# Seeding a second accumulation by a PSUM-to-PSUM copy in a seven-product matmul kernel

## The chip, the cores and the metric

The kernel runs on one core of one Trainium2 chip. The metric is the device time of one execution in microseconds (us). The engines are PE (TensorE, matrix products), DVE (VectorE), ACT (ScalarE), POOL (GpSimd) and SP (SyncE, which here only issues DMAs). PE writes its products to PSUM, a small memory of eight banks per partition, from which DVE and ACT read them.

## The reference, cut to what matters

A linear attention gives x of 4608 tokens by 512. Two blocks follow, each with its own float64 weights of 512 x 2048 and 2048 x 512:

```python
def _moe_ref(x, w_in, w_out):
    h = x @ w_in
    r = np.maximum(h, 0.0)
    return (r * r @ w_out).astype(np.float32)

def _moe2_ref(x, w_in, w_out):
    h = x @ w_in
    return ((h * np.cos(h)) @ w_out).astype(np.float32)
```

## The kernel before, in words

Every product is made of three PE passes: each operand is split into a high and a low part, and high x high, high x low and low x high are summed in PSUM. A first stage (up to 499 us) does the attention and one half of the first block in plain tiles. The second stage is a list of 30 `slots`, numbered k = 0 to 29 in the order of work. A slot is (m, t, q): m is the block (0 or 1), t one of five token tiles, q a group of hidden features. Tiles 0 to 2 have 2 x 512 tokens and tiles 3 and 4 have 2 x 384. Slots 0 to 9 belong to block 0 (two groups a tile), slots 10 to 29 to block 1 (four groups a tile). Slots 10, 14, 18, 22 and 26 begin a new tile of block 1 (q = 0), and the input blocks of the tile are made around them.

In a slot the product x @ w_in is done as seven products of 2 x 2 blocks instead of eight (`first_product`, indices i of `ORDER` = 0, 1, 3, 2, 5, 4, 6, each of 12 matmuls). They go to two double banks, `FA` and `FB`, of 128 x 2 x 512 float32: 0, 3, 5 and 6 to one, 1, 2 and 4 to the other, the roles changing from slot to slot. Some accumulate on what the bank holds: 3 on 0, 5 on those, 4 on 2. Block (0, 0) of h is product 0 plus product 1: ACT copies product 0 to SBUF (`keep`, tile `m`) and DVE adds product 1 from the other bank (`add`, L530 or L534). The four blocks then go through a chain that ACT and DVE share (`relu_1`, `relu_2`, or `cos_1` to `cos_5`). The last block, (1, 0), comes from product 6 at the slot's end.

The result of the chain is multiplied by w_out, again by seven products in most slots (`second_product`, banks `SA` and `SB`, matmuls of 256 columns in block 1, 24 of them to a product in tiles of 2 x 512 tokens and 18 in tiles of 2 x 384). Their order is `S_ORDER`. `s_block` makes the operand of each: a difference of blocks where needed (tiles `t`), then the high part `gh` on ACT and the low part `gl` on DVE. `drain_product` adds each product to a sum in SBUF: at q = 0 of block 1 four of them by an ACT copy that starts the sum, otherwise by a DVE add (L700), and products 4, 5, 1 and 6 (`BY_DMA`) by an ACT copy to one of two `part` buffers and a DMA that adds it to the sum (L697, L698). The second products of slot k run 1.25 slots after its first ones, so PE alternates between first products of slot k + 1 and second products of slot k.

`run_slots` sets the order by a clock of steps: step n issues one matmul of the first products, and as many of the second products as are due at n/84 slots. All other work hangs in a list of jobs by position (`at(pos(...))`, unit PH = 1/7 slot), and a scheduler puts each engine's instructions in a queue that it works off in order.

Of the kernel before, what the change touches and what calls it, by code (L numbers as in the profile page):

```python
# [8 lines left out]
F32 = mybir.dt.float32  # L9
# [13 lines left out]
def kernel(  # L23
# [15 lines left out]
    nc = tc.nc  # L39
# [390 lines left out]
    ORDER = (0, 1, 3, 2, 5, 4, 6)  # L430
    W_OF = (0, 1, 3, 4, 6, 5, 2)
    BLOCKS = {(0, 0): 2, (1, 1): 5, (0, 1): 6, (1, 0): 7}
    S_ORDER = (0, 2, 3, 4, 5, 1, 6)
    BY_DMA = (4, 5, 1, 6)
    xb, wi, wo, kept, hs, ys, sums, quads = {}, {}, {}, {}, {}, {}, {}, {}

    def big(pool, dtype, name, ht):
# [62 lines left out]
    def first_product(k, i):  # L500
        m, t, q = slots[k]
        ps = f_bank(k, i)
        w, x = wi[k, i], xb[m, t, i]
        for pp in range(2):
            n = 0
            for j in range(2):
                wh, wl = (w[:, a, pp, j, :] for a in range(2))
                xh, xl = (y[:, j, :] for y in x)
                for a, b in ((wh, xh), (wh, xl), (wl, xh)):
                    nc.tensor.matmul(  # L510
                        ps[:, pp, :], a, b, start=(i in (0, 1, 2) and n == 0), stop=(n == 5), skip_group_check=True
                    )
                    n += 1
                    yield

    def scale_of(k):
        return -INV_2PI if slots[k][0] else 1.0

    def t_tile(k, dtype, name):
        return big("c", dtype, name, TILES[slots[k][1]][1])  # L520
# [12 lines left out]
        else:  # L533
            nc.vector.tensor_tensor(out=h, in0=f_bank(k, i), in1=t, op=ALU.add)  # L534

    def last(k):
        hs[k, (1, 0)] = h = t_tile(k, F32, "h")
        m = slots[k][0]
        nc.scalar.activation(out=h, in_=f_bank(k, 6), func=AF.Copy if m else AF.Relu, scale=scale_of(k))  # L539

    def relu_1(k, b):
        if b != (1, 0):
            nc.scalar.activation(out=hs[k, b], in_=hs[k, b], func=AF.Relu)

    def relu_2(k, b):
# [80 lines left out]
    def s_block(k, i):  # L626
        m, t, q = slots[k]
        b11, b12, b21, b22 = (ys.get((k, b)) for b in ((0, 0), (0, 1), (1, 0), (1, 1)))

        def minus(out, x, y):  # L630
            nc.vector.tensor_tensor(out=out, in0=x, in1=y, op=ALU.subtract)
            return out

        if i == 2:
            ys[k, "t1"] = minus(t_tile(k, F32, "t"), b12, b11)
        if i == 3:
            ys[k, "t2"] = minus(t_tile(k, F32, "t"), b22, ys[k, "t1"])
        src = {
            0: lambda: b11,
            1: lambda: b21,  # L640
            2: lambda: ys[k, "t1"],
            3: lambda: ys[k, "t2"],
            4: lambda: b22,
            5: lambda: minus(b12, b22, b12),
            6: lambda: minus(b21, b21, ys[k, "t2"]),
        }[i]()
        gs[k, i] = h, l = [t_tile(k, F32R, f"g{n}") for n in "hl"]
        nc.scalar.copy(out=h, in_=src)  # L648
        nc.vector.tensor_tensor(out=l, in0=src, in1=as32(h), op=ALU.subtract)  # L649
# [9 lines left out]
    def second_product(k, i):  # L659
        m, t, q = slots[k]  # L660
        ps = blocks_of(t, s_bank(k, i), m)
        w, g = wo.pop((k, i)), gs.pop((k, i))
        nb = TILES[t][1] // P if m else 2
        for b in range(nb):
            n = 0
            for pp in range(2):
                for x, y in ((0, 0), (0, 1), (1, 0)):
                    if m == 0:
                        lhs, rhs = w[:, x, pp, b, :], g[y][:, pp, :]
                    else:  # L670
                        lhs, rhs = g[y][:, pp, b * P:(b + 1) * P], w[:, x, pp, :, :].rearrange("p i n -> p (i n)")
                    nc.tensor.matmul(  # L672
                        ps[:, b, :],
                        lhs,
                        rhs,
                        start=(i in (0, 1, 2) and n == 0 and (m == 0 or b % 2 == 0)),
                        stop=(n == 5),
                        skip_group_check=True,
                    )
                    n += 1  # L680
                    if n == 6 and b == nb - 1:
                        drain_product(k, i)
                    yield
# [3 lines left out]
    def drain_product(k, i):  # L687
        m, t, q = slots[k]
        ps, (d, j) = blocks_of(t, s_bank(k, i), m), SUM_OF[i]
        if q == 0 and m and i in (0, 2, 3, 6):  # L690
            sums[m, t, d, j] = e = w_p.tile([P, 2, 512], F32, tag="w", name="sum")
            nc.scalar.copy(out=blocks_of(t, e), in_=ps)
        else:
            e = blocks_of(t, sums[m, t, d, j], m)
            if m and i in BY_DMA and k < len(slots) - 1:
                part = blocks_of(t, conv_p.tile([P, 2, 512], F32, tag="raw", name="part"))
                nc.scalar.copy(out=part, in_=ps)  # L697
                nc.gpsimd.dma_start(out=e, in_=part, accum_op=ALU.add)  # L698
            else:
                nc.vector.tensor_tensor(out=e, in0=ps, in1=e, op=ALU.add)  # L700
        if m and q == groups_of[m][-1] and i in (4, 5, 1, 6):
            t0, ht = TILES[t]
            dst = out[t0 + j * ht:t0 + (j + 1) * ht, 2 * P * d:2 * P * (d + 1)]
            delay = 0.25 if k < len(slots) - 1 else 0
            later(delay, nc.sync.dma_start, out=dst.rearrange("(b p) n -> p b n", p=P), in_=e)
# [90 lines left out]
    for k, (m, t, q) in enumerate(slots):  # L796
        if q == 0:
            for a in range(2):
                at(pos(k + (a - 6.8) * PH) if k else nA0 - 9, load_quads, m, t, a)
            for f, i in enumerate(ORDER):  # L800
                at(pos(k + X_AT[f] * PH) if k or f > 3 else nA0 - 7 + 1.5 * f, x_block, k, i)
        for f, i in enumerate(ORDER):
            at(pos(k + (f - 2.7) * PH) if k or f > 2 else nA0 - 5 + f / 2, load_wi, k, i)
        if (m, q) in seven:
            for f, i in enumerate(S_ORDER):
                at(pos(k + LAG2 + (f - 2.7) * PH), load_ws, k, i)
                at(pos(k + LAG2 + (f - 1.6) * PH), s_block, k, i)
        else:
            for a, c in enumerate(CHUNKS):
                at(pos(k + LAG2 - 0.4 + a / 8), load_wo, k, c)  # L810
        at(pos(k + 1 * PH), keep, k, "m1", 0)
        at(pos(k + 2 * PH), add, k, (0, 0), 1, "m1")
        at(pos(k + 3 * PH), keep, k, "u2", 3)
        at(pos(k + 4 * PH), keep, k, "m5", 2)
        at(pos(k + 5 * PH), add, k, (1, 1), 5, "m5")
        at(pos(k + 6 * PH), add, k, (0, 1), 4, "u2")
        at(pos(k + 7 * PH), last, k)
        chain = ((cos_1, cos_2, cos_3, cos_4, cos_5) if m else (relu_1, relu_2)) + (() if (m, q) in seven else (g_hi, g_lo))
        for b, f in BLOCKS.items():
            for a, fn in enumerate(chain):  # L820
                at(pos(k + (f + 0.25 * (a + 1)) * PH), fn, k, b)
        if m == 0 and q == 0:
            for n, dj in enumerate(((0, 0), (1, 1), (0, 1), (1, 0))):
                at(pos(k + LAG2 + (n - 2) * PH), load_sum, k, *dj)
# [36 lines left out]
    def run_slots():  # L861
        nonlocal here
        size = [
            42 * (TILES[t][1] // P if m else 2) if (m, q) in seven else 12 * len(units(k)) for k, (m, t, q) in enumerate(slots)
        ]
        seconds = [k + LAG2 + n / size[k] for k in range(len(slots)) for n in range(size[k])]
        firsts = [(k, i) for k in range(len(slots)) for i in ORDER]
        steps1 = (x for k, i in firsts for x in first_product(k, i))
        todo = [
            (second_product, k, i) if slots[k][0::2] in seven else (second, k, i)  # L870
            for k in range(len(slots))
            for i in (S_ORDER if slots[k][0::2] in seven else range(len(units(k)) // 4))
        ]
        steps2 = (x for fn, *a in todo for x in fn(*a))
        nf, ns = 12 * len(firsts), 0
        n = 0
        while n < nf or ns < len(seconds):
            here = n / 84
            run_pending()
            run_jobs(nA0 + here)  # L880
            while ns < len(seconds) and seconds[ns] <= here:
                next(steps2)
                ns += 1
            if n < nf:
                next(steps1)
            n += 1
        here = float("inf")
        run_pending()
        run_jobs(here)
# [83 lines left out]
```

## Time and profile before

| | |
|---|---|
| median of 3 runs | 1583.31 us (1581.37 to 1585.13) |
| the profiled execution | 1582.0 us, span 1580.2 us from first to last instruction |
| PE busy | 1547.6 us (98%) |
| DVE busy | 1256.6 us (80%) |
| ACT busy | 1060.5 us (67%) |
| granted TensorE clock | 1.000 of full speed, mean |
| DMA queue of loads and stores (q1) | 73.1% of 16 engines' span |

The engines work side by side. A busy share says how long an engine had an instruction under way, not that it set the end; what sets the end is read stretch by stretch from what the engine that never rests waits for.

### The profile page before, as it was taken

To read this page: it belongs to the slowest core of one execution; us is meant where nothing else is said; L and a number is where in the kernel's file an instruction comes from. 1 tells how busy PE (TensorE), PEld (TensorE's weight loads), DVE (VectorE), ACT (ScalarE), POOL (GpSimd) and SP (SyncE) were. 2 spreads that over 40 slices of the span, in tenths; PEclk is the share of its full clock that TensorE was granted. 3 is DMA by queue.
4 is the path that set the end of the run, shared out by engine and by line. 5 is a ranking of instruction groups with operands and counts; after the bars stand their busy time and mean duration, and the time that the engine had idled before them with its cause. 6 is when DMAs were issued, how large, how long until landed. Compare 5 with 4: busy or idle time off the path is not lost.

```text
span 1580.2 us, 24826 instructions
## 1 busy us (share of the span) xinstructions
PE 1547.6 (98%) x9164; PEld 1356.4 (86%) x9164; DVE 1256.6 (80%) x1714; ACT 1060.5 (67%) x1515; POOL 115.4 (7%) x125
## 2 busy tenths in 40 slices
PE   5999999999999999999999999999999999999998
PEld 3777777778887878888999899999999999999998
DVE  7988878788874888889847678967896788689777
ACT  5977777775443756565645667776777677777774
POOL 1100201111100000000000000000000001101110
PEclk9999999999999999999999999999999999999999
DMA  8858879866667889999987679998899789999995
GB/s 317 282 158 243 263 235 278 240 202 207 185 219 256 298 271 336 302 335 330 374 281 291 246 213 270 266 277 246 267 260 291 230 260 290 277 363 314 284 351 164
DMA packets 236999, 425.53 MB, mean 269 GB/s; under 512 B 18512, under 2 KB 155216, under 8 KB 236880
## 3 DMA queue, kind: packets, MB, share of 16 engines
q1 hardware_dynamic: 225888, 387.78, 73.1%
q0 software_dynamic: 10992, 36.18, 11.4%
q8 instruction: 73, 1.20, 0.3%
q14 instruction: 46, 0.38, 0.1%
HBM read 309.85 MB, written 80.22 MB: 247 GB/s over the span
## 4 chain that ended last, share of the span: by engine, by line
PE 79%; DVE 8%; DMA 7%; issue 3%; ACT 2%; SPq 1%; POOL 0%; DVEq 0%; POOLq 0%; ACTq 0%
PE FA L510 14%; PE FB L510 14%; PE SA L672 12%; PE SB L672 12%; PE acc L422 10%; PE l L385 9%; PE SB L609 2%; PE SA L609 2%; DMA wi_d<-raw 2%; DMA raw<-in_wB 2%; PE o L385 1%; DMA sum<-part 1%; PE ss L385 1%; DMA ws_d<-raw 1%; DVE gl L649 1%
## 5 line engine op out<-in xcount | busy, mean ns | idle before, releaser
L510 PE MATMUL FA<-xh,wi 128*128 128x512 f32 (+1 forms) x840 | 306.0, 370 | 1.9 <-issue 1.0
L510 PE MATMUL FB<-xh,wi 128*128 128x512 f32 (+1 forms) x840 | 305.4, 370 | 0.0
L672 PE MATMUL SB<-ws,gh 128*128 128x256 f32 x1008 | 237.9, 280 | 1.1 <-ACT u L524 0.7
L672 PE MATMUL SA<-ws,gh 128*128 128x256 f32 x1008 | 237.9, 280 | 0.0
L672 PEld LDWEIGHTS SB<-ws,gh 128*128 128x128 f32 x1008 | 186.0, 188 | 14.4 <-ACT u L524 1.0
L672 PEld LDWEIGHTS SA<-ws,gh 128*128 128x128 f32 x1008 | 186.2, 188 | 13.2
L510 PEld LDWEIGHTS FA<-xh,wi 128*128 128x128 f32 x840 | 157.7, 188 | 12.1 <-issue 1.4
L510 PEld LDWEIGHTS FB<-xh,wi 128*128 128x128 f32 x840 | 157.8, 188 | 8.3 <-ACT h L539 0.3
L649 DVE TENSOR_TENSOR gl<-y,gh 128x1024 fp32r<-128x1024 f32 (+1 forms) x100 | 111.4, 1114 | 38.7 <-ACT gh L648 38.5
L672 PE MATMUL SA<-ws,gl 128*128 128x256 f32 x504 | 141.0, 280 | 1.1 <-DVE gl L649 1.1
L672 PE MATMUL SB<-ws,gl 128*128 128x256 f32 x504 | 141.2, 280 | 0.8 <-DVE gl L649 0.7
L698 POOL DMA_DIRECT2D sum<-part x71 | 60.3, 850 | 1093.4 <-ACT part L697 1078.6
L569 DVE SCALAR_TENSOR_TENSOR y<-y,h 128x1024 f32<-128x1024 f32 (+1 forms) x80 | 89.1, 1114 | 53.5 <-ACT y L565 53.2
L551 ACT ACTIVATE y<-h,zerob 128x1024 int32<-128x1024 f32 (+1 forms) x80 | 85.1, 1064 | 50.5 <-DVE h L530 50.5
L422 PE MATMUL acc<-gh,wh 128*128 128x512 f32 x288 | 113.6, 395 | 0.0
L422 PE MATMUL acc<-gl,wh 128*128 128x512 f32 x288 | 112.9, 392 | 0.0
L422 PE MATMUL acc<-gh,wl 128*128 128x512 f32 x288 | 112.6, 391 | 0.0
L510 PE MATMUL FA<-xl,wi 128*128 128x512 f32 (+1 forms) x300 | 111.0, 370 | 0.0
L510 PE MATMUL FB<-xl,wi 128*128 128x512 f32 (+1 forms) x300 | 110.9, 370 | 0.0
L672 PEld LDWEIGHTS SB<-ws,gl 128*128 128x128 f32 x504 | 94.7, 188 | 7.9 <-DVE gl L649 1.5
L672 PEld LDWEIGHTS SA<-ws,gl 128*128 128x128 f32 x504 | 94.7, 188 | 7.9 <-DVE gl L649 1.3
L385 PE MATMUL l<-xh,wh 128*128 128x512 f32 x240 | 96.6, 403 | 2.1 <-ACT xh L354 1.2
(181 smaller groups left out, 3773.4 us busy)
## 6 DMA issues: line engine op xcount, KB each, us to landing
wi<-wi_d SPq DMA_DIRECT2D x210, 512.0 KB, 7.0
ws<-ws_d SPq DMA_DIRECT2D x175, 512.0 KB, 5.9
sum<-part POOLq DMA_DIRECT2D x45, 512.0 KB, 7.6
kvld<-in_kv SPq DMA_DIRECT2D x32, 512.0 KB, 6.8
wi_d<-wh SPq DMA_DIRECT2D x24, 448.0 KB, 4.3
wi_d<-raw SPq DMA_DIRECT2D x24, 448.0 KB, 4.7
raw<-in_wA SPq DMA_DIRECT2D x20, 512.0 KB, 6.4
wo<-wo_d SPq DMA_DIRECT2D x20, 512.0 KB, 8.2
```

The costliest lines, as they stand in the source:

```text
L385: nc.tensor.matmul(ps, a[:, 0, cs], m[:], start=(c == 0 and k == 0), stop=(c == NKC - 1 and k == 2))
L422: nc.tensor.matmul(o, a[:, cs], m[:], start=(f == 0 and n == 0), stop=(f == NH - 1 and n == 2), skip_group_check=True)
L510: nc.tensor.matmul(ps[:, pp, :], a, b, start=(i in (0, 1, 2) and n == 0), stop=(n == 5), skip_group_check=True)
L551: nc.scalar.activation(out=y.bitcast(I32), in_=hs[k, b], func=AF.Identity, bias=zerob)
L569: nc.vector.scalar_tensor_tensor(out=y, in0=y, scalar=-2.0 * math.pi, in1=hs.pop((k, b)), op0=ALU.add, op1=ALU.mult)
L609: nc.tensor.matmul(ps, lhs, rhs, start=(a == 0 and (x, y) == (0, 0)), stop=last, skip_group_check=True)
L649: nc.vector.tensor_tensor(out=l, in0=src, in1=as32(h), op=ALU.subtract)
L672: nc.tensor.matmul(ps[:, b, :], lhs, rhs, start=(i in (0, 1, 2) and n == 0 and (m == 0 or b % 2 == 0)), stop=(n == 5), skip_group_check=True,)
L698: nc.gpsimd.dma_start(out=e, in_=part, accum_op=ALU.add)
```

## The change

From slot 2 on (`SEEDED`), where the slot's tile is not longer than that of the slot before, product 0 is copied by ACT from its bank into the other bank (`seed`), product 1 accumulates on that copy, and one ACT instruction (`whole`) takes the finished block (0, 0) out. That concerns 27 slots (2 to 29 without 10). The second products do the same with their products 0 and 1 in 22 of them (`seeded_s`), for which `S_ORDER` becomes 0, 1, 3, 2, 5, 4, 6. PE must not touch either bank while the copy runs, so `HOLD` = 9 of the 12 steps of product 1 are held back: the other stream of products runs alone meanwhile, and the 12 matmuls follow in the last three steps.

```diff
-    S_ORDER = (0, 2, 3, 4, 5, 1, 6)
+    S_ORDER = (0, 1, 3, 2, 5, 4, 6)
+    SEEDED = 2
+    def seeded(k):
+        return k >= SEEDED and TILES[slots[k][1]][1] <= TILES[slots[k - 1][1]][1]
+    def seeded_s(k):
+        return seeded(k) and k < len(slots) - 1
+    HOLD = 9
...
+                        start=(n == 0 and (i in (0, 2) or i == 1 and not seeded(k))),
...
-    def last(k):
-        hs[k, (1, 0)] = h = t_tile(k, F32, "h")
+    def seed(k):
+        nc.scalar.copy(out=f_bank(k, 1), in_=f_bank(k, 0))
+    def whole(k, b, i):
+        hs[k, b] = h = t_tile(k, F32, "h")
         m = slots[k][0]
-        nc.scalar.activation(out=h, in_=f_bank(k, 6), func=AF.Copy if m else AF.Relu, scale=scale_of(k))
+        nc.scalar.activation(out=h, in_=f_bank(k, i), func=AF.Copy if m else AF.Relu, scale=scale_of(k))
...
-        if i == 2:
+        if i == 3:
             ys[k, "t1"] = minus(t_tile(k, F32, "t"), b12, b11)
-        if i == 3:
             ys[k, "t2"] = minus(t_tile(k, F32, "t"), b22, ys[k, "t1"])
...
-        if q == 0 and m and i in (0, 2, 3, 6):
+        if i == 0 and seeded_s(k):
+            nc.scalar.copy(out=blocks_of(t, s_bank(k, 1), m), in_=ps)
+            return
+        if q == 0 and m and i in (1 if seeded_s(k) else 0, 2, 3, 6):
...
-                at(pos(k + LAG2 + (f - 1.6) * PH), s_block, k, i)
+                at(pos(k + LAG2 + (f - (1.1 if f == 1 else 1.6)) * PH), s_block, k, i)
...
-        at(pos(k + 1 * PH), keep, k, "m1", 0)
-        at(pos(k + 2 * PH), add, k, (0, 0), 1, "m1")
+        if not seeded(k):
+            at(pos(k + 1 * PH), keep, k, "m1", 0)
+            at(pos(k + 2 * PH), add, k, (0, 0), 1, "m1")
+        else:
+            at(pos(k + 1 * PH), seed, k)
+            at(pos(k + 2 * PH), whole, k, (0, 0), 1)
...
+            if seeded(k) and 12 <= j < 24:
+                j = 24 - (24 - j) * (12 - HOLD) / 12
```

Three places of the new order matter. In all of them `FA`, `FB`, `SA`, `SB` are the PSUM double banks, `wi` and `ws` weights, and a number after a name tells buffers apart.

PE in slot 16, where product 0 (bank `FA`) ends and product 1 (bank `FB`) begins, before:

```order
L510 MATMUL FA<-xh,wi 128x512
L672 MATMUL SA<-ws,gh 128x256 x2
L510 MATMUL FB<-xh,wi 128x512
L672 MATMUL SA<-ws,gl 128x256
L672 MATMUL SA<-ws,gh 128x256
```

The same place in the changed kernel:

```order
L519 MATMUL FA<-xh,wi 128x512
L688 MATMUL SA<-ws,gh 128x256 x2
L688 MATMUL SA<-ws,gl 128x256
...
L688 MATMUL SA<-ws,gl 128x256
L688 MATMUL SA<-ws,gh 128x256
L688 MATMUL SB<-ws,gh 128x256
L519 MATMUL FB<-xh,wi 128x512
```

Between the two products stand 20 matmuls of 256 columns now, where two stood. In slots 14, 18 and 26 they are 24, in slots 24, 25 and 27 to 29 they are 15, of the same kind.

ACT in slot 29, from the copy of a second product (`part`, product 4 or 1) ahead of the slot's product 0 on, before:

```order
L697 COPY part_15618<-SA_5836 128x768
L524 ACTIVATE m1_15632<-FB_5835 128x2x384
L561 ACTIVATE y_15600<-y_15600 128x2x384
L648 CAST gh_15641<-t_15639 128x2x384
L565 ACTIVATE y_15600<-y_15600 128x2x384
L697 COPY part_15666<-SB_5837 128x768
L648 CAST gh_15687<-t_15685 128x2x384
L551 ACTIVATE y_15696<-h_15678,zerob_69 128x2x384
```

And changed:

```order
L716 COPY part_15576<-SA_5836 128x768
L551 COPY FA_5834<-FB_5835 128x2x384
L578 ACTIVATE y_15558<-y_15558 128x2x384
L582 ACTIVATE y_15558<-y_15558 128x2x384
L716 COPY part_15612<-SB_5837 128x768
L664 CAST gh_15606<-y_15558 128x2x384
L556 ACTIVATE h_15633<-FA_5834 128x2x384
L664 CAST gh_15644<-t_15642 128x2x384
L707 COPY SB_5837<-SA_5836 128x768
L568 ACTIVATE y_15653<-h_15633,zerob_69 128x2x384
```

The two new copies (L551 for the first products, L707 for the second) stand in ACT's queue, the second behind the `part` copy of product 6, behind `gh` of block (1, 0) and behind `gh` of the difference t.

DVE at the end of the program, from the first operand of the last slot's second products on, before (block (1, 0) is `y_15915`):

```order
L649 TENSOR_TENSOR gl_15908<-y_15696,gh_15907 128x2x384
L631 TENSOR_TENSOR t_15940<-y_15872,y_15696 128x2x384
L555 SCALAR_TENSOR_TENSOR y_15915<-y_15915,h_15900 128x2x384
L631 TENSOR_TENSOR y_15872<-y_15824,y_15872 128x2x384
L649 TENSOR_TENSOR gl_15943<-t_15940,gh_15942 128x2x384
L631 TENSOR_TENSOR t_15970<-y_15824,t_15940 128x2x384
L569 SCALAR_TENSOR_TENSOR y_15915<-y_15915,h_15900 128x2x384
```

And changed (block (1, 0) is `y_15872`):

```order
L665 TENSOR_TENSOR gl_15865<-y_15653,gh_15864 128x2x384
L572 SCALAR_TENSOR_TENSOR y_15872<-y_15872,h_15857 128x2x384
L719 TENSOR_TENSOR sum_15067<-SB_5837,sum_15067 128x768
L586 SCALAR_TENSOR_TENSOR y_15872<-y_15872,h_15857 128x2x384
L665 TENSOR_TENSOR gl_15908<-y_15872,gh_15907 128x2x384
L648 TENSOR_TENSOR t_15925<-y_15829,y_15653 128x2x384
L648 TENSOR_TENSOR t_15927<-y_15783,t_15925 128x2x384
```

The low part of block (1, 0), which product 1 needs, is now the second operand to be made, ahead of both differences t, and the drain of product 0 (L719) stands within its chain.

## Rows read from the trace of the kernel before

**Rows 1.** The page, busy time of each engine:
```profile
PE 1547.6 (98%) x9164; PEld 1356.4 (86%) x9164; DVE 1256.6 (80%) x1714; ACT 1060.5 (67%) x1515; POOL 115.4 (7%) x125
```

**Rows 2.** Busy time by stretch (from:to in us, its length, then engines):
```profile
core 0: us, PE busy (x) PEld busy (x) DVE busy (x) ACT busy (x) POOL busy (x), PEclk, DMA share, GB/s
552.99:842.33 289.34, 288.01 (x1393) 252.49 (x1392) 240.40 (x312) 165.45 (x189) 0.00 (x0) 1.00 0.94 323
878.55:1309.12 430.57, 430.57 (x2755) 390.58 (x2755) 344.99 (x298) 314.52 (x322) 32.30 (x39) 1.00 0.86 257
1309.12:1575.60 266.48, 263.51 (x1891) 261.85 (x1889) 209.60 (x229) 193.93 (x247) 28.04 (x33) 1.00 0.94 295
594.35:633.69 39.34, 39.04 (x173) 32.02 (x172) 36.68 (x41) 26.07 (x28) 0.00 (x0) 1.00 0.96 332
```

**Rows 3.** What PE waited for from 499 us on, longest waits (total us, times, longest):
```profile
PE SA L672 <- DVE gl L649: 1.1, 1, 1.1
PE FA L510 <- issue: 1.0, 1, 1.0
PE SB L672 <- DVE gl L649: 0.7, 2, 0.5
PE SB L672 <- ACT u L524: 0.7, 1, 0.7
PE SA L672 <- issue: 0.5, 2, 0.3
```

**Rows 4.** The chain that ended last (start, us, engine, tile):
```profile
508.73 2.72 PE FB L510 x12
...
730.05 2.10 PE FA L510 x12
...
1573.43 2.17 PE SB L672 x18
```

**Rows 5.** Timeline, slot 17: last matmul of product 0, and ACT's copy of it:
```profile
1118.26 0.40 PE L510 MATMUL FB<-xh,wi 128*128 128x512 f32 x1
...
1118.69 1.03 ACT L524 ACTIVATE m<-FB 128x1024 f32<-128x1024 f32 x1 [0.17 <-PE FB L510]
```

**Rows 6.** Timeline, the same in slots 18 and 26, in 18 with ACT's instruction before:
```profile
1157.45 0.40 PE L510 MATMUL FA<-xh,wi 128*128 128x512 f32 x1
...
1160.15 1.07 ACT L561 ACTIVATE y<-y 128x1024 f32<-128x1024 f32 x1
1161.11 1.02 ACT L524 ACTIVATE m<-FA 128x1024 f32<-128x1024 f32 x1
...
1437.62 0.34 PE L510 MATMUL FA<-xh,wi 128*128 128x384 f32 x1
...
1441.36 0.81 ACT L524 ACTIVATE m<-FA 128x768 f32<-128x768 f32 x1
```

**Rows 7.** Timeline of ACT, slots 23 and 24: two `part` copies to one buffer:
```profile
1369.48 0.80 ACT L697 COPY part<-SB 128x768 f32<-128x768 f32 x1 [1.23 <-PE SB L672]
...
1376.68 0.83 ACT L648 CAST gh<-y 128x768 fp32r<-128x768 f32 x1
...
1379.51 0.80 ACT L697 COPY part<-SB 128x768 f32<-128x768 f32 x1 [1.17 <-DMA sum<-part]
```

**Rows 8.** Timeline, the end: last first product, block (1, 0), the second operand:
```profile
1553.33 0.34 PE L510 MATMUL FB<-xh,wi 128*128 128x384 f32 x1
...
1554.27 0.79 ACT L539 ACTIVATE h<-FB 128x768 f32<-128x768 f32 x1
...
1559.84 0.28 PE L672 MATMUL SA<-ws,gh 128*128 128x256 f32 x1
...
1561.18 0.39 PE L672 MATMUL SA<-ws,gl 128*128 128x256 f32 x1 [1.07 <-DVE gl L649]
...
1561.91 0.95 DVE L569 SCALAR_TENSOR_TENSOR y<-y,h 128x768 f32<-128x768 f32 x1
```

**Rows 9.** DVE's adds of product 1 from 842 us on, by form (count, busy us, mean ns):
```profile
L530 DVE SCALAR_TENSOR_TENSOR h<-FA,m 128x1024 f32<-128x1024 f32 x12 | 14.7, 1222 | 1.1 <-PE FA L510 0.8
```

More of the change, by code (lines that the diff above doesn't have):

```diff
@@ L510, in first_product @@
                     nc.tensor.matmul(
-                        ps[:, pp, :], a, b, start=(i in (0, 1, 2) and n == 0), stop=(n == 5), skip_group_check=True
+                        ps[:, pp, :],
+                        a,
+                        b,
+                        start=(n == 0 and (i in (0, 2) or i == 1 and not seeded(k))),
+                        stop=(n == 5),
+                        skip_group_check=True,
                     )
@@ L534, in add @@
             nc.vector.tensor_tensor(out=h, in0=f_bank(k, i), in1=t, op=ALU.add)
-    def last(k):
-        hs[k, (1, 0)] = h = t_tile(k, F32, "h")
+    def seed(k):
+        nc.scalar.copy(out=f_bank(k, 1), in_=f_bank(k, 0))
+    def whole(k, b, i):
+        hs[k, b] = h = t_tile(k, F32, "h")
         m = slots[k][0]
-        nc.scalar.activation(out=h, in_=f_bank(k, 6), func=AF.Copy if m else AF.Relu, scale=scale_of(k))
+        nc.scalar.activation(out=h, in_=f_bank(k, i), func=AF.Copy if m else AF.Relu, scale=scale_of(k))
     def relu_1(k, b):
-        if b != (1, 0):
+        if b != (1, 0) and (b != (0, 0) or not seeded(k)):
             nc.scalar.activation(out=hs[k, b], in_=hs[k, b], func=AF.Relu)
@@ L675, in second_product @@
                         rhs,
-                        start=(i in (0, 1, 2) and n == 0 and (m == 0 or b % 2 == 0)),
+                        start=(n == 0 and (m == 0 or b % 2 == 0) and (i in (0, 2) or i == 1 and not seeded_s(k))),
                         stop=(n == 5),
@@ L816 @@
         at(pos(k + 6 * PH), add, k, (0, 1), 4, "u2")
-        at(pos(k + 7 * PH), last, k)
+        at(pos(k + 7 * PH), whole, k, (1, 0), 6)
         chain = ((cos_1, cos_2, cos_3, cos_4, cos_5) if m else (relu_1, relu_2)) + (() if (m, q) in seven else (g_hi, g_lo))
@@ L865, in run_slots, with held @@
         ]
-        seconds = [k + LAG2 + n / size[k] for k in range(len(slots)) for n in range(size[k])]
+        def held(x):
+            return 2 * PH - (2 * PH - x) * (12 - HOLD) / 12 if PH <= x < 2 * PH else x
+        seconds = [
+            k + LAG2 + (held(n / size[k]) if slots[k][0::2] in seven and seeded_s(k) else n / size[k])
+            for k in range(len(slots))
+            for n in range(size[k])
+        ]
         firsts = [(k, i) for k in range(len(slots)) for i in ORDER]
@@ L875, in run_slots @@
         nf, ns = 12 * len(firsts), 0
-        n = 0
-        while n < nf or ns < len(seconds):
+        due = []
+        for n in range(nf):
+            k, j = divmod(n, 84)
+            if seeded(k) and 12 <= j < 24:
+                j = 24 - (24 - j) * (12 - HOLD) / 12
+            due.append(k * 84 + j)
+        n = done1 = 0
+        while done1 < nf or ns < len(seconds):
             here = n / 84
@@ L883, in run_slots @@
                 ns += 1
-            if n < nf:
+            while done1 < nf and due[done1] <= n:
                 next(steps1)
+                done1 += 1
             n += 1
```

## The prediction

> **What bounds the kernel now.** I read the page's busy times first: PE is busy for 1547.6 of 1580.2 us, DVE for 1256.6, ACT for 1060.5 [rows 1]. A share of 98% could still hide a slow stretch, so I read the busy time by stretch next. From 878.55 to 1309.12 PE has an instruction under way for all 430.57 us; from 552.99 to 842.33 it is idle for 289.34 - 288.01 = 1.3 us, from 1309.12 to the end for 266.48 - 263.51 = 3.0 us [rows 2]. The reader is to see that the second stage has 1.3 + 0 + 3.0 = 4.3 us of idle PE to give back in those stretches, and that in the middle one, 12 slots long, no other engine matters.
>
> The list of PE's waits says where the idle time is: single waits of about 1 us or less, for a low part `gl` (1.1 and 0.7 us), for a block's copy (0.7 us), and one of 1.0 us in slot 0, which the change does not reach [rows 3]. Last, the chain of waits gives PE's issue prices, since for most of its length it is PE alone: 12 matmuls of 512 columns take 2.72 us (0.227 each), 12 of 384 take 2.10 (0.175), 18 of 256 take 2.17 (0.12) [rows 4]. A slot of 512 tokens in block 1 is 84 x 0.227 + 168 x 0.12 = 39.2 us, one of 384 is 84 x 0.175 + 126 x 0.12 = 29.8 us at most. The change leaves every matmul in place, so these sums stay. What counts is only idle time of PE, added or taken away. A difference of 0.2%, or 3.2 us, is about what a measurement of this kernel can tell from none.
>
> **Work moved between engines: -0.5 us.** DVE loses 27 adds of product 1 and 18 adds of second products, at 1.22 us in slots of 512 tokens [rows 9] and 0.95 in those of 384 (as the op in rows 8); the adds of four more seeded second products had been made by DMA. In slot 3 DVE is busy for 36.68 of 39.34 us [rows 2], so there the relief can shorten a wait; but PE idles for only 0.3 us in it, and for 1.3 us in the whole stretch of block 0. I take 0.5 of the 1.3. In block 1 DVE is busy for 344.99 of 430.57 us while PE never rests, so less DVE work buys nothing there: PE's own matmuls are the cover, and would have to go for it to count. The Trainium skill says (Perfetto Trace Analysis, "Optimizing Scalar/DVE Operations") that moving work from DVE to ScalarE may help where DVE is saturated. The trace agrees that DVE is near that in slot 3, and shows the opposite in block 1; by the rule applied to all slots the result would be the second rival below.
>
> **Seeds of the first products: +1.2 us.** PE may not start product 1 before the copy has landed. Nothing before copies from PSUM to PSUM, so its price is bounded by ACT's copy of the same tile to SBUF, 1.03 us [rows 5], and by DVE's 1.22 us for an op that also reads PSUM [rows 9]; I take the first, since engine, input and shape are the same. In slot 17 the copy started 0.43 us after the start of product 0's last matmul (1118.26 to 1118.69) and would end 1.46 us after it [rows 5]. Until product 1 is due, PE has that matmul and 20 of the other stream: 0.23 + 20 x 0.12 = 2.63 us. The copy is hidden with 1.2 us to spare, at the DVE price with 1.0. In slots of 384 the cover is 0.175 + 15 x 0.12 = 1.98 us against about 0.43 + 0.8. So nothing for most of the 27.
>
> Two places differ. In slots 18 and 26 ACT was late: its copy ran from 3.66 to 4.68 us after the last matmul began in the one, from 3.74 to 4.55 in the other [rows 6]. In 18 an instruction of 1.07 us ran just ahead of it; the new order puts that one behind the seed, and its like in 26 (some 0.8 us there, as the ACT rows of that size in rows 7), so the seeds should end at about 3.6 and 3.7. The cover of 24 matmuls is 0.23 + 24 x 0.12 = 3.1 us: waits of 0.5 and 0.7, together +1.2. Low end 0, where ACT's queue has drained; high end 4, where the other slots that begin a tile are as late.
>
> **Seeds of the second products: +3 us.** The cover here is the nine held matmuls: 9 x 0.227 = 2.04 us at 512 tokens, 9 x 0.175 = 1.57 at 384. The copy takes 1.46 and 1.23 us with its delay, by the same rows, so in an empty queue it is hidden, with 0.6 and 0.3 us left. But ACT's queue isn't empty. At 384 the seed stands behind the `part` copy of product 6, two `gh` and the block's copy. Two `part` buffers serve products 1, 5, 4, 6 in the new order, so product 6 takes the buffer of product 5. How long a buffer is taken is seen before: copied from 1369.48, it was waited for until 1379.51, 10.0 us from start to start [rows 7]. Product 6 now follows 5 by two products, 2 x 29.8/7 = 8.5 us, less the 9 x 0.175 = 1.6 us by which the held steps bring it forward: 6.9 us. Its copy may thus be 3.1 us late, and the seed behind it starts after 0.80 + 0.83 + 0.79 + 0.83 us more, 13.3 us after product 5's copy, where it was wanted 6.9 + 4.3 = 11.2 us after it. Late by 2.1, less the 0.3 in reserve: 1.8 us at worst. The full queue stands before the seeds of slots 25, 26 and 28. 10.0 us is one hold, seen in one place, so I take about half, 1.0 us each: +3 for the three. The ends are 0 (sums land faster) and 8 (all seven seeds of that size late by over 1 us).
>
> **A wait that goes: -0.9 us.** In slot 26 PE waited 0.7 us for ACT's copy `u`, and 0.2 for a `gl` behind it (the lesser of two, 0.7 in all with 0.5 the longest) [rows 3]. ACT's queue is reordered there, and the first-product burst after the hold moves the needed time back. What is late next is that slot's seed, counted above.
>
> **The tail: +4.0 us.** In slot 29 the second products have no seed and nothing beside them. Product 1 is now second, and its operand is block (1, 0), the last to be made. The last first product began at 1553.33, the block was copied from 1554.27, and its chain ended at 1561.91 + 0.95 = 1562.86 [rows 8]. `gh` (0.83) and `gl` (0.95) follow, so it is complete at about 1564.7. PE's second operand was due at 1559.84, and the product went on at 1561.18, once `gl` had come [rows 8]. If the chain keeps its pace, that is 4.8 us of waiting. The differences t1 and t2 (0.95 each) stand behind it on DVE and then need `gh` and `gl`, so product 3 waits too, some 1.6 us. Sum 6.4, less the waits that are there already: 1.1 and 0.5 [rows 3] and smaller ones of some 0.8, so about +4.0. Low end 1.5: without the two `part` copies of 0.80 and DVE's differences ahead of it the chain from 1555.06 is four ACT instructions of 0.83 (three of the chain, and `gh`) and two of 0.95 on DVE, and `gh` is there at 1560.3. High end 5.
>
> **Sum.** -0.5 - 0.9 + 1.2 + 3.0 + 4.0 = +6.8 us. The profiled execution, 1582.0 us (span 1580.2), would become 1588.8. It lies 1.3 under the median of the runs, so 1583.3 + 6.8 = **1590.1 us**.
>
> **Rivals.** *Everything is covered.* The `part` buffers come free in time, ACT catches up in slots 18 and 26, and the tail is at its low end: 0 to +3, **1583 to 1586 us**. For it: PE's cover is longer than the copy nearly everywhere. Against it: DVE's order at the end, which the change writes down.
>
> *Faster.* The 45 adds gone from DVE take away the 1.3 us of block 0 and the late `gl`s, and the tail's chain, with DVE emptier, is done by the time its operand is due. The point that decides is 1559.84: are both parts of block (1, 0) ready then? If so, up to 4.3 us are won: **1579 us**. For it: DVE ran differences between the links of that chain, which now come after it. Against it: even the chain without any of these gives `gh` at 1560.3.
>
> *Heavy.* Each of the 49 seeds is late by some 0.5 us, because a copy into PSUM takes over 2 us, or ACT falls behind at every product: + 25, **1608 us**. It decides at a copy of about 1.6 us in the second products. Against it: 0.8 to 1.03 for every copy from PSUM in the trace [rows 5 to 7].
>
> *The clock falls.* The granted clock is 1.00 in every stretch, also in those where PE waited [rows 2]. If the waits at the seeds brought the lower of the two levels (1.2 instead of 2.4 GHz) for one product after each, 2.72 us would become 5.44: 49 x 2.72 = +133, **about 1716 us**. The Trainium skill has such a rule (TensorE: Matmul & The Clock Gate, "A second HAM failure mode: psum-queue depth-cycling"): small idle times between PSUM groups let the clock swing. No stretch here shows it.
>
> That the seed were overwritten and not added to would change the numbers computed, but no time.
>
> **How the numbers follow.** Forecast (1586.5 to 1600): 0.53. Covered: 0.27. Faster: 0.12. Heavy: 0.07. Clock: 0.01. The forecast's own bounds are -1.3 - 0.9 + 0 + 0 + 1.5 = -0.7 and 0 + 0 + 4 + 8 + 5 = +17; the range 1580.5 to 1600 takes in the covered case, half of the faster one and nearly all of the forecast. Faster by over 0.2% (under 1580.1): 0.12. Within 0.2% (to 1586.5): the covered case and a little of its neighbours, 0.28. Slower: 0.60.
>
> **What would show it.** In the changed profile slots of 512 tokens in block 1 stay at 39.2 us; PE's waits on ACT at the first matmul of product 1 appear in slots 18 and 26 alone; the second products wait for ACT only in the last slots of 384, where a `part` copy ahead of the seed waits for a DMA; and after 1554 PE waits 4 to 6 us for `gh` and `gl` of block (1, 0). I am wrong if PE's idle time after the last first product is under 3 us, if slots of 512 grow by 0.5 us or more (heavy), or if the granted clock leaves 1.00.

## The result, and the profile after

The changed kernel takes 1599.6 us (median of 4 runs, 1598.05 to 1600.89) against 1582.62 us before: a ratio of 1.0105, 95% interval 1.0087 to 1.0122. It is 17 us slower, where 6.8 were forecast. The profiled execution has a span of 1597.9 us, 17.7 more than before, and is used below.

The page, busy time of each engine, against [rows 1]:

```profile
PE 1554.1 (97%) x9164; PEld 1360.1 (85%) x9164; DVE 1211.6 (76%) x1669; ACT 1092.3 (68%) x1552; POOL 112.1 (7%) x121
```

The work moved as meant: 45 instructions and 45 us have left DVE, ACT has 32 us more, PE has the same 9164 matmuls. Busy time by stretch, for the same slots as in [rows 2] (2 to 9, 11 to 21, 22 to the end; a slot is counted from its first first-product matmul to that of the next slot):

```profile
core 0: us, PE busy (x) PEld busy (x) DVE busy (x) ACT busy (x) POOL busy (x), PEclk, DMA share, GB/s
554.67:845.81 291.14, 287.28 (x1394) 252.60 (x1393) 229.87 (x301) 168.00 (x193) 0.00 (x0) 1.00 0.94 322
882.06:1314.78 432.72, 432.66 (x2756) 391.56 (x2755) 322.42 (x279) 332.77 (x341) 30.60 (x37) 1.00 0.85 254
1314.78:1593.30 278.52, 268.51 (x1891) 264.65 (x1889) 198.17 (x215) 204.50 (x261) 26.35 (x31) 0.99 0.90 279
```

Three different losses show. The first stretch is 1.8 us longer, with 3.9 us of idle PE for 1.3. The second is 2.2 us longer (432.72 for 430.57) though PE never rests: its busy time itself has grown. The third is 12.0 us longer (278.52 for 266.48), of it 10.0 us idle for 3.0, and 5.0 us more busy time, with a granted clock no longer at 1.00. The start of the second stage (500.6 for 499.3 us) and slot 0 add the remaining 1.7; the start differs as much in the runs below, in either direction (498.3 to 502.0).

PE's waits from 499 us on, against [rows 3]:

```profile
PE SA L688 <- ACT gh L664: 3.8, 2, 2.8
PE SB L688 <- ACT SB L707: 2.8, 2, 2.5
PE SB L626 <- DVE sum L639: 2.6, 1, 2.6
PE SA L688 <- DVE gl L665: 1.6, 3, 0.6
PE FA L519 <- ACT h L556: 1.4, 1, 1.4
```

The three longest lead to three places. **The end** (slot 29 up to the start of its last matmul, 56.29 us for 51.22): the timeline of ACT, DVE and PE, second products now at L688.

```profile
1573.20 0.84 ACT L582 ACTIVATE y<-y 128x768 f32<-128x768 f32 x1
1573.29 0.96 DVE L719 TENSOR_TENSOR sum<-SB,sum 128x768 f32<-128x768 f32 x1 [1.00 <-PE SB L688]
1574.16 0.95 DVE L586 SCALAR_TENSOR_TENSOR y<-y,h 128x768 f32<-128x768 f32 x1
1575.15 0.83 ACT L664 CAST gh<-y 128x768 fp32r<-128x768 f32 x1 [1.11 <-DVE y L586]
...
1576.03 0.38 PE L688 MATMUL SA<-ws,gh 128*128 128x256 f32 x1 [2.78 <-ACT gh L664]
...
1577.02 0.58 PE L688 MATMUL SA<-ws,gl 128*128 128x256 f32 x1 [0.61 <-DVE gl L665]
```

The reader sees the chain of block (1, 0): its last step L586, its high part, and PE that waited 2.78 us for that. The drain of product 0 (L719) runs on DVE just ahead of L586, but L582 ended only at 1574.04, so it cost the chain no more than some 0.1 us.

**Slot 23** (35.13 us for 30.78): ACT's timeline. L716 is the `part` copy of product 6, L707 the seed.

```profile
1360.54 1.01 ACT L716 COPY part<-SB 128x1024 f32<-128x1024 f32 x1 [3.67 <-DMA sum<-part]
1361.45 0.84 ACT L664 CAST gh<-y 128x768 fp32r<-128x768 f32 x1
1362.18 0.81 ACT L556 ACTIVATE h<-FA 128x768 f32<-128x768 f32 x1
1365.24 0.83 ACT L664 CAST gh<-t 128x768 fp32r<-128x768 f32 x1 [2.24 <-DVE t L648]
1365.98 0.79 ACT L707 COPY SB<-SA 128x768 f32<-128x768 f32 x1
```

The `part` copy waited 3.67 us for the DMA that was emptying its buffer. `gh` behind it came late, so did `gl` and the differences `t` behind it in DVE's queue, and the seed stands behind the `gh` of such a `t`. PE waited 2.46 us for the seed, until 1366.83. Then the granted clock fell. Busy time of three stretches right after (a count takes in every instruction under way in the stretch):

```profile
1366.90:1368.30 1.40, 1.40 (x11) 1.40 (x12) 1.40 (x3) 1.40 (x3) 0.00 (x0) 1.00 1.01 293
1368.40:1371.70 3.30, 3.30 (x16) 3.30 (x16) 2.20 (x3) 3.04 (x4) 0.00 (x0) 0.50 0.61 205
1371.80:1375.20 3.40, 3.40 (x26) 3.40 (x25) 0.96 (x1) 1.53 (x2) 0.00 (x0) 1.00 1.02 354
```

PE's timeline, a matmul of 256 columns and the next one in the second of these stretches, and the same in the third:

```profile
1369.48 0.41 PE L688 MATMUL SB<-ws,gl 128*128 128x256 f32 x1
1369.69 0.63 PE L688 MATMUL SB<-ws,gh 128*128 128x256 f32 x2
...
1372.81 0.28 PE L688 MATMUL SA<-ws,gl 128*128 128x256 f32 x1
1372.93 0.34 PE L519 MATMUL FB<-xh,wi 128*128 128x384 f32 x1
```

In the middle one PE was at the lower of its two levels (1.2 GHz, granted 0.50), and a matmul of 256 columns took 0.21 us from its start to the next; after it, at 2.4 GHz, 0.12. The clock record holds the low level for 3.4 us. In it 14 matmuls began, 11 of 256 columns and 3 of 384; at the rates of the mixture (0.118 and 0.175 us) they would have taken 1.5 us less. So one such fall costs about 1.5 us on top of the wait. A second one follows the wait of 2.78 us at the end.

**Slot 2** (44.78 us for 41.35): DVE's timeline, first in the changed kernel, then the two instructions before.

```profile
584.72 1.22 DVE L548 TENSOR_TENSOR h<-FA,m 128x1024 f32<-128x1024 f32 x1
...
589.99 0.43 DVE L119 TENSOR_SCALAR e<-raw 128x512 uint32<-128x512 uint32 x1 [4.05 <-DMA raw<-in_wB]
590.33 1.22 DVE L639 TENSOR_TENSOR sum<-SB,sum 128x1024 f32<-128x1024 f32 x1
```

```profile
584.12 1.22 DVE L622 TENSOR_TENSOR sum<-SB,sum 128x1024 f32<-128x1024 f32 x1 [0.30 <-PE SB L609]
586.27 0.43 DVE L119 TENSOR_SCALAR e<-raw 128x512 uint32<-128x512 uint32 x1 [0.93 <-DMA raw<-in_wB]
```

L639 drains bank `SB` (L622 before), and PE waited 2.62 us for it. It now stands behind L119, the first step of a weight conversion, which waited 4.05 us for its load. Before, the drain stood ahead of that step. The scheduler swapped the two.

The copies themselves cost what was expected. Groups of ACT from 842 us on, by form:

```profile
L707 ACT COPY SA<-SB 128x1024 f32<-128x1024 f32 x6 | 6.0, 1002 | 4.2 <-PE SB L688 4.2
L551 ACT COPY FA<-FB 128x1024 f32<-128x1024 f32 x6 | 6.0, 999 | 0.8 <-PE FB L519 0.8
...
L707 ACT COPY SB<-SA 128x768 f32<-128x768 f32 x4 | 3.2, 801 | 0.0
```

A copy from PSUM to PSUM takes 1.00 and 0.80 us, as much as the copies to SBUF [rows 5 to 7].

### The profile page after: what moved, and what is told of

Its sections match the earlier page's. It is cut to its first block, busy times and chain, and to the rows that moved or that the text cites. A ratio compares the mean times of both kernels' runs of the same rounds, so it can differ in the third digit from the quotient of the medians.

```text
span 1597.9 us, 24852 instructions
## 1 busy us (share of the span) xinstructions
PE 1554.1 (97%) x9164; PEld 1360.1 (85%) x9164; DVE 1211.6 (76%) x1669; ACT 1092.3 (68%) x1552; POOL 112.1 (7%) x121
## 4 chain that ended last, share of the span: by engine, by line
PE 79%; DMA 8%; DVE 6%; issue 4%; ACT 3%; SPq 1%; DVEq 0%; ACTq 0%; POOLq 0%
PE FB L519 13%; PE FA L519 13%; PE SA L688 12%; PE SB L688 11%; PE acc L422 11%; PE l L385 9%; DMA sum<-part 3%; PE SA L626 2%; PE SB L626 2%; DMA raw<-in_wB 2%; PE o L385 1%; DMA wi_d<-raw 1%; DMA ws_d<-raw 1%; DVE gl L665 1%; PE ss L385 1%
## 5 line engine op out<-in xcount | busy, mean ns | idle before, releaser
L519 PE MATMUL FA<-xh,wi 128*128 128x512 f32 (+1 forms) x840 | 300.2, 371 | 3.5 <-ACT h L556 1.4
L519 PE MATMUL FB<-xh,wi 128*128 128x512 f32 (+1 forms) x840 | 300.1, 371 | 0.0
L688 PE MATMUL SA<-ws,gh 128*128 128x256 f32 x1008 | 230.5, 282 | 3.8 <-ACT gh L664 3.8
L688 PE MATMUL SB<-ws,gh 128*128 128x256 f32 x1008 | 229.4, 282 | 2.9 <-ACT SB L707 2.8
L688 PEld LDWEIGHTS SA<-ws,gh 128*128 128x128 f32 x1008 | 182.4, 190 | 15.5 <-ACT gh L664 4.1
L688 PEld LDWEIGHTS SB<-ws,gh 128*128 128x128 f32 x1008 | 180.9, 189 | 14.8 <-ACT SB L707 4.2
L586 DVE SCALAR_TENSOR_TENSOR y<-y,h 128x1024 f32<-128x1024 f32 (+1 forms) x80 | 89.2, 1116 | 109.9 <-ACT y L582 109.8
L519 PEld LDWEIGHTS FA<-xh,wi 128*128 128x128 f32 x840 | 157.3, 188 | 15.8 <-ACT h L556 1.7
L519 PEld LDWEIGHTS FB<-xh,wi 128*128 128x128 f32 x840 | 157.3, 188 | 11.3 <-ACT FB L551 0.2
L688 PE MATMUL SA<-ws,gl 128*128 128x256 f32 x504 | 142.5, 283 | 1.6 <-DVE gl L665 1.6
L688 PE MATMUL SB<-ws,gl 128*128 128x256 f32 x504 | 142.2, 282 | 0.5 <-DVE gl L665 0.5
L717 POOL DMA_DIRECT2D sum<-part x67 | 56.9, 850 | 1108.8 <-ACT part L716 1029.0
L519 PE MATMUL FA<-xl,wi 128*128 128x512 f32 (+1 forms) x300 | 111.2, 371 | 0.0
L519 PE MATMUL FB<-xl,wi 128*128 128x512 f32 (+1 forms) x300 | 110.9, 370 | 0.0
L664 ACT CAST gh<-y 128x1024 fp32r<-128x1024 f32 (+1 forms) x100 | 94.9, 960 | 12.6 <-DVE y L586 7.6
L688 PEld LDWEIGHTS SA<-ws,gl 128*128 128x128 f32 x504 | 95.8, 190 | 7.9 <-DVE gl L665 2.3
L688 PEld LDWEIGHTS SB<-ws,gl 128*128 128x128 f32 x504 | 95.4, 189 | 6.5 <-DVE gl L665 1.1
```

The source lines that it names most:

```text
L519: nc.tensor.matmul(ps[:, pp, :], a, b, start=(n == 0 and (i in (0, 2) or i == 1 and not seeded(k))), stop=(n == 5), skip_group_check=True,)
L586: nc.vector.scalar_tensor_tensor(out=y, in0=y, scalar=-2.0 * math.pi, in1=hs.pop((k, b)), op0=ALU.add, op1=ALU.mult)
L688: nc.tensor.matmul(ps[:, b, :], lhs, rhs, start=(n == 0 and (m == 0 or b % 2 == 0) and (i in (0, 2) or i == 1 and not seeded_s(k))), stop= ...
```

## The experiments

Theory A: the loss sits in four places (the tail, the `part` buffer ahead of a seed, slot 2, and the clock's falls behind them) and in a drift of 0.16 us a slot. Theory B: each seed, or each hold, costs PE time by itself.

**Seeds of the first products alone (e1).** The second products keep the old order and drains:

```diff
-    S_ORDER = (0, 1, 3, 2, 5, 4, 6)
+    S_NEW, S_OLD = (0, 1, 3, 2, 5, 4, 6), (0, 2, 3, 4, 5, 1, 6)
+    def s_order(k):
+        return S_OLD
...
     def seeded_s(k):
-        return seeded(k) and k < len(slots) - 1
+        return False
...
-            for f, i in enumerate(S_ORDER):
+            for f, i in enumerate(s_order(k)):
```

> Only the first products are seeded (27 copies, with the hold of product 1); the second products keep their old order and their old drains. Theory A (the loss sits in the late operands at the end, in the part copies that wait for a DMA ahead of a seed, and in one wait in slot 2): the tail and the part waits of before come back, so 1582.6 us plus some 0.16 us a slot and perhaps the 3 us of slot 2: 1583 to 1588 us. Theory B (each seed or hold costs PE time by itself): 27 of 49 copies are left, so over half of the 17 us stays: 1592 to 1597 us.

Measured: 1589.14 us, ratio 1.0041 (1.0029 to 1.0053). Slot 29 is back at 51.24 us, slot 23 at 30.73; slot 2 keeps its loss (45.63, with a fall of the clock), and most slots of 512 tokens take 39.28 us. So 27 of the 49 copies bring 6.2 of the 17 us, and 4.3 us of that is slot 2. The time lies between the two ranges, 1.1 us above theory A's and 2.9 below theory B's; the places speak for A. But PE also waited for a seed here, 0.3 us each in slots 24 and 28.

**The order alone (e2).** No seed and no hold:

```diff
-    SEEDED = 2
+    SEEDED = 99
```

> No seed and no hold at all; only the second products' order is the new one (0, 1, 3, 2, 5, 4, 6). Theory A: the tail keeps its 5 us (block (1, 0) is the second operand there too), the part waits keep a part of theirs because products 5 and 6 still share a buffer, but nothing stands behind them for PE: 1587 to 1592 us. Theory B: without copies the loss is gone: 1582 to 1584 us.

Measured: 1597.25 us, ratio 1.0088 (1.0075 to 1.0101), so 14 us without a single seed: against theory B, and 5 us more than theory A allowed. PE's waits at the end, those from 995 to 1340 us, and DVE in slot 14:

```profile
PE SA L688 <- ACT gh L664: 3.7, 2, 2.8
```

```profile
PE SB L688 <- DVE gl L665: 3.2, 3, 1.9
```

```profile
1009.30 1.22 DVE L544 SCALAR_TENSOR_TENSOR h<-FB,m 128x1024 f32<-128x1024 f32 x1
...
1011.57 1.22 DVE L719 TENSOR_TENSOR sum<-SB,sum 128x1024 f32<-128x1024 f32 x1
...
1016.10 1.22 DVE L665 TENSOR_TENSOR gl<-t,gh 128x1024 fp32r<-128x1024 f32 x1
```

The tail is that of the changed kernel (56.41 us). What I had not seen is that slots 14, 18 and 22 each take 1.7 to 2.2 us more: where a tile begins, the operand of product 3, now the third one, is late. Its low part is made from a difference `t`, and in DVE's queue the add of product 1 (L544) and the drain of product 0 (L719) stand ahead of that. The seeds take both away: in the changed kernel this `gl` ends 20.4 us after the start of slot 14, for 22.4 here, and PE does not wait for it. So the parts of the change don't add up: e1 and e2 cost 6.2 and 14.3 us, the whole change 17. The median lies 4.5 us over the profiled execution (1592.8), and the runs spread from 1592.8 to 1601.1; how much of that spread is the clock no trace tells, since only one execution has one.

**The old order in the last slot alone (e3).**

```diff
-    S_ORDER = (0, 1, 3, 2, 5, 4, 6)
+    S_NEW, S_OLD = (0, 1, 3, 2, 5, 4, 6), (0, 2, 3, 4, 5, 1, 6)
+    def s_order(k):
+        return S_NEW if k < len(slots) - 1 else S_OLD
...
-            for f, i in enumerate(S_ORDER):
+            for f, i in enumerate(s_order(k)):
```

> The changed kernel with the old order of the second products in the last slot alone. Theory A: the waits after the last first product fall from 7.8 to some 2.7 us, so 1599.6 - 5 = 1594 to 1595 us. Rival: the drains and operands of slot 28 are late all the same, and the wait only moves: 1598 to 1600 us.

Measured: 1594.82 us, ratio 1.0067 (1.0055 to 1.0079): 4.8 us less than the changed kernel, slot 29 at 51.92. The tail is shown.

**A buffer of its own for product 6 (e4)**, in tiles of 384 tokens:

```diff
+                if t > 2 and i == 6:
+                    part = pools["part"].tile([P, 2 * TILES[t][1]], F32, tag="part", name="part")
...
+                else:
+                    part = blocks_of(t, conv_p.tile([P, 2, 512], F32, tag="raw", name="part"))
...
+    pools["part"] = ctx.enter_context(tc.tile_pool(name="part", bufs=1, side="left"))
```

> The changed kernel with a part buffer of its own for product 6 in the tiles of 384 tokens, so that its copy no longer waits for the DMA that adds product 5. Theory A: ACT's waits for that DMA go (11.6 us in six places) and with them PE's waits in slots 23, 25 and 27, some 7 us with the clock's fall in slot 23: 1592 to 1594 us. Rival: the seed in slot 23 stands behind the high part of a difference that DVE made late, and that is late anyway: 1598 to 1600 us.

Measured: 1597.75 us, ratio 1.009 (1.0077 to 1.0103), only 1.9 us less, and outside both ranges. The slots tell why: 25, 26 and 27 went from 30.41, 30.07 and 32.07 to 29.58, 29.68 and 29.58 us, 3.7 us together. But slot 23 kept its wait (2.4 us for the seed): the `part` copy ahead of it belongs to slot 21, of 512 tokens, still shared a buffer, and again waited 3.70 us for its DMA. And slots 2 and 29 were 2.0 and 1.3 us longer than in the changed kernel's trace, each with a fall of the clock, at 29 one of 10.2 us. The mechanism is shown for slot 27 alone, which keeps 31.80 and 31.61 us in e3 and e5, where the buffer is still shared, and takes 29.58 again in e6; slots 25 and 26 take 29.58 and 29.73 to 29.81 us there too, so what they gain here is no more than traces differ. The size was wrong for want of slot 23.

**Seeds from slot 3 on (e5).**

```diff
-    SEEDED = 2
+    SEEDED = 3
```

> The changed kernel with SEEDED = 3, so that slot 2 alone keeps its old copy and add. With it the add that drains bank SB stands again ahead of a step of the weight conversion (L119) that waits for a load; with a seed in slot 2 it stood behind. Theory A: PE's 2.6 us wait for that drain goes, and with it the clock's fall that followed it in three of five profiles (1.7 us each): 3 to 5 us less than 1599.6, so 1594.5 to 1597 us. Rival (the swapped place is a symptom, slot 2 is late for loads in any case): slot 2 keeps its 44 us and the time stays at 1598 to 1600 us.

Measured: 1596.31 us, ratio 1.009 (1.0074 to 1.0105), 3.3 us less. DVE's timeline at the same place:

```profile
585.38 1.23 DVE L639 TENSOR_TENSOR sum<-SB,sum 128x1024 f32<-128x1024 f32 x1 [0.31 <-PE SB L626]
587.09 0.43 DVE L119 TENSOR_SCALAR e<-raw 128x512 uint32<-128x512 uint32 x1 [0.49 <-DMA raw<-in_wB]
```

The drain runs 1.7 us ahead of L119, and slot 2 takes 42.07 us. Slots 3 and 5 were 1.0 and 1.1 us longer in this trace, so part of the gain is given back there.

**All four repairs together (e6).** The edits of the last three, and slot 21's product 6 drained by a DVE add:

```diff
-            if m and i in BY_DMA and k < len(slots) - 1:
+            if m and i in BY_DMA and k < len(slots) - 1 and (i, k) != (6, 21):
```

> The changed kernel with all four places mended: seeds from slot 3, old order in the last slot, a part buffer of its own for product 6 in tiles of 384 tokens, and in slot 21 product 6 drained by a DVE add instead of a part copy. 46 of 49 seeds or more stay. Theory A (four places and a drift of 0.16 us a slot are the whole loss): 1582.9 + 20 x 0.16 - 1.7 (block 0) - 1.3 (slot 26) = 1583 us, 1581.5 to 1585. Theory B (seeds and holds cost by themselves): over 1590 us.

Measured: 1585.7 us, ratio 1.0022 (1.0012 to 1.0031). With 47 of the 49 seeds in place 14 of the 17 us are gone. Slot 23 is back at 30.80 us, where e3, e4 and e5, each with one of the other edits, left it at 34.62, 33.65 and 32.56; so the `part` copy of slot 21's product 6 is what made its seed late. What is left, 3.1 us, is not the drift of 0.16 us in 20 slots that I had put down: slots 12 to 22 hold 2.2 us of it, while slots 24, 25, 27 and 28, of 384 tokens, are only 0.3 us longer together. PE's longest waits from 499 us on:

```profile
PE SA L693 <- DVE sum L643: 2.4, 2, 1.8
PE SA L693 <- DVE gl L670: 1.1, 1, 1.1
PE FA L523 <- issue: 1.0, 1, 1.0
```

No seed is among them any more. The time is 0.7 us over my bound. Theory B falls as an account of the 17 us; a small price of the hold stays, as the next run shows.

**The hold without copies (e7).** Old copy and add, old order, but nine steps of product 1 held, in the 27 slots of the changed kernel (`SEEDED` stayed at 2, so slot 2 is among them, unlike what I expected below; it took 41.43 us for 41.35):

```diff
     def seeded(k):
+        return False
+    def held_f(k):
         return k >= SEEDED and TILES[slots[k][1]][1] <= TILES[slots[k - 1][1]][1]
...
-            if seeded(k) and 12 <= j < 24:
+            if held_f(k) and 12 <= j < 24:
```

> No seeds; the old copy and add, the old order of the second products; but the nine steps of product 1 are held back in the same 26 slots (3 to 29 without 10) as with seeds. Theory A: the drift belongs to PE's order, not to the copies: slots 12 to 21 take 39.28 us as with first-product seeds alone, and the time is 1582.9 + 20 x 0.08 = 1584 to 1585 us. Rival (the copy into PSUM slows PE's neighbouring matmuls): slots of 39.20 us and 1582 to 1583.5 us.

Measured: 1583.83 us, ratio 1.001 (1.0001 to 1.0019). The time lies between theory A's range and the rival's, within 0.4 us of both, so the slots decide: nine of the ten from 12 to 21 take 39.28 us (18 took 40.31, with a wait of 0.8 us behind a `part` copy). Slot 12, without a copy:

```profile
916.04:955.32 39.28, 39.28 (x255) 35.63 (x254) 29.54 (x25) 26.56 (x28) 2.56 (x4) 1.00 0.78 225
```

The drift of 0.08 us is there with PE never idle and no seed: it belongs to PE's order. The starts of matmuls in slot 16 say where it arises. In the mixture 256 columns take 117 to 119 ns and 512 take 229 to 233; where the hold lets the second products run alone most take 120, and where first products catch up side by side they take 233 on average, for 231 in the mixture. These two stretches hold some 0.05 of the 0.08 us.

**A hold of five steps (e11)**, HOLD = 5 in the last kernel.

> e7 with five steps held instead of nine. Theory A (the drift comes from matmuls of one kind standing next to each other, 256-column ones 2 to 3 ns and 512-column ones some 4 ns longer than in the mixture): fewer stand together, slots 12, 13, 16 and 17 take 39.23 to 39.25 us instead of 39.28. Rival (a fixed price of a hold): 39.28 us.

Measured in one profile: slots 12 to 16 and 18 to 21 take 39.25 us (17 took 39.51). That is theory A's number: the drift follows the length of the hold. The hold of the second products, to which the other 0.08 us of the changed kernel's 0.16 would belong, was not run by itself.

**Attempts at something faster (e8, e9, e10).** Block 0 alone, `return SEEDED <= k < 10 and ...` with SEEDED = 3 and the old order:

> First products seeded in slots 3 to 9 alone, where DVE was near saturated; block 1 and the second products as before. Theory A: slots 3 to 9 lose some 1.2 us, as they did with first-product seeds alone, and the rest stays: 1581 to 1582.5 us, just under before. Rival (the adds taken from DVE there free nothing): 1582.5 to 1584 us.

Measured: 1581.7 us, ratio 0.9997 (0.9987 to 1.0007). The time is in theory A's range, but no difference to the kernel before can be seen, so the run does not decide. Then the six slots that were shorter in the hold without copies, with the hold alone and with seeds (`return k in (4, 5, 6, 7, 8, 26)` in `held_f` or in `seeded`):

> The kernel before with the hold of product 1, without copies, in slots 4 to 8 and 26 alone: the slots that were shorter in e7 than before (by 0.9, 0.4, 0.1, 0.1, 0.1 and 1.2 us). Theory A (a held product 1 gives late operands time, and costs 0.08 us only where PE never waits): the 2.7 us come together, 1582.6 - 2.7 = 1580 us. Rival (those differences are run-to-run differences of loads): 1582 to 1583.5 us.

> The same six slots with the seeding copies of the first products too; second products as before. Theory A: the copy adds nothing to the hold here, 1580 to 1581 us, equal to e9 within 1 us. Rival (taking the add of product 1 from DVE is what helped in block 0): over 1 us faster than e9.

Measured: 1583.02 us, ratio 0.9997 (0.9988 to 1.0005), and 1581.94 us, ratio 0.999 (0.998 to 1.000). Neither gains what was expected: theory A's 2.7 us is refuted. Slot 5 took 40.71 us with the hold alone, and 39.25 in the trace from which I had chosen it. A slot of block 0 differs by 1 us and more from trace to trace, with its loads, and I had read one trace of each as a gain. Whether the seeds beat the hold alone by 1 us stays open. No version beats the kernel before by more than its measurement is uncertain.

## Why the prediction was wrong

The direction was right, and so was the mechanism of the two largest terms; the time lies inside the range by 0.4 us. The size was off by a factor of 2.5. Three steps failed: the term for the seeds of the second products was too small (3.0, measured 7.8), a swap in DVE's queue was put at nothing (3.4), and PE's own sums were taken as fixed (2.5). Step by step, by the profiled execution:

- **What bounds the kernel.** PE does bound it. But "The change leaves every matmul in place, so these sums stay" is the first step that failed: the same matmuls in another order take 39.36 us a slot in the changed kernel, 39.28 with one hold and 39.20 in the mixture. Over slots 10 to 22 it is +2.5 us. The hint was in [rows 4]: 18 matmuls of a second product alone take 2.17 us, 0.1206 each, more than the 117 to 119 ns they take in the mixture. I used one rounded price for both. (The middle stretch is 11 slots long, not 12.)
- **Work moved between engines, -0.5.** Unresolved in size: slots 3 to 9 were 1.6 us shorter, but e8 shows no gain from seeds there.
- **A swap that is not in the sum.** I counted instructions on DVE and did not follow what their places had become. In slot 2 a drain went behind a step that waits for a load: +3.4 us. The order of the built program already holds the swap.
- **Seeds of the first products, +1.2.** Too high. In the slot I had named, PE (L519) and ACT show it:

```profile
1162.31 0.40 PE L519 MATMUL FA<-xh,wi 128*128 128x512 f32 x1
...
1165.42 0.50 PE L519 MATMUL FB<-xh,wi 128*128 128x512 f32 x1
```

```profile
1164.36 1.01 ACT L551 COPY FB<-FA 128x1024 f32<-128x1024 f32 x1
```

  The seed of slot 18 ended 3.06 us after the last matmul of product 0 began (estimate 3.6), product 1 started at 3.11 us, as the cover of 3.1 said. The copy hid by 0.05 us. PE's list of waits has no seed of a first product in it, neither here nor in slot 26.
- **Seeds of the second products, +3 (0 to 8).** The mechanism is right, `part` copies that wait for a DMA ahead of a seed (11.6 us in six places, 4.7 in four before). The term was mis-sized, and the places were wrong: slots 23, 25 and 27 grew by 4.4, 0.9 and 2.5 us, 7.8 together. I had the full queue before the seeds of slots 25, 26 and 28, and of these PE waited for the last alone, 0.4 us. I overlooked slot 22's, which falls into slot 23 and stands behind a copy of 512-token size; its late `t` and the clock's fall made it the dearest. In slot 27 PE waited 1.4 us not for the seed but for block (0, 0)'s copy (L556), queued behind a late `part` copy, and there and in slot 25 0.5 us for a `gl`; slot 25's growth is not in every trace (e3, e5).
- **A wait that goes, -0.9.** Right: -1.2 in slot 26.
- **The tail, +4.0 (1.5 to 5).** The mechanism is right and the size is +5.1. The waits are 2.78 + 0.61 us for block (1, 0), against 4.8 estimated, and about 1.4 for product 3's operands, against 1.6; the fall of the clock brings some 1.5 us more. So it is partly luck that the number is close: all waits of the slot grew by 3.3 us only, and the clock made up for it.
- **The clock.** As an all-or-nothing rival it was rightly put low. But the granted clock did leave 1.00, one of my signs of being wrong: it fell twice, for 3.4 us each, some 3 us that no term holds. The Trainium skill (TensorE: Matmul & The Clock Gate, "A second HAM failure mode: psum-queue depth-cycling") tells of a clock that swings between its two levels because PE is idle for short times, often, between groups of matmuls. The trace agrees in part: the clock moved between the same two levels, but each fall came after a single wait of over 2 us (2.46 and 2.78).
- **The "heavy" rival** is refuted: a copy takes 1.00 us, and of the 49 seeds PE waited for two (2.46 and 0.35 us).

Together: 1.7 (start and slot 0) + 1.8 (slots 2 to 9) + 2.5 (10 to 22) + 6.8 (23 to 28) + 5.0 (29 to the end of the program) = 17.8, against 17.7 measured.

## What to carry to other kernels

When an edit goes through a scheduler, compare each engine's order around the instructions that wait for a load or a buffer: one drain moved behind one load-waiting step cost 3.4 us, about as much as 47 seeds with their holds (3.1). Put the operand that is finished last at the end of the last stage's order. Do not price a PE-bound stretch by its count of matmuls alone, and where a wait of PE of some 2 us is to be expected, count a low-clock stretch behind it as likely.

## What was unexpected of the hardware

The granted clock fell to half after nine of the eleven waits of 2.0 to 2.8 us that PE had in the second stage of the changed kernel and of e1 to e5, mostly for 3.4 us; in two of the nine (e4 and e5, at the end) for 10.2 us. It did not fall after any of those between 1.0 and 1.94 us. Within one execution two waits of 2.62 and 2.46 us differ: in the changed kernel the first (slot 2) left the clock at 1.00 and the second (slot 23) brought it down; in e4 waits of 2.62 and 2.44 us at the same two places did the opposite. What decides between them these runs do not show.
